# Swapping two of the seven products in a retention + PReLU kernel

## The chip, the cores and the metric

The kernel runs on one core of one Trainium2 chip. The metric is the device time of one execution in microseconds (us). Before the change the median of three runs is 198.67 us (197.17 to 201.42). The engines are named as the profile names them: PE multiplies matrices into PSUM banks, PEld loads its weights, DVE, ACT and POOL work element by element, SP starts most DMAs. Each engine takes its instructions in the order in which the program issues them.

## The reference

For each of 4 batches and 8 heads a retention state is carried through 768 steps; its output, as 3072 rows of 512 columns, goes through a two-layer network with a PReLU between:

```python
gamma = 1.0 - 2.0 ** (-5.0 - np.arange(H))
for t in range(S):                       # B, H, S, D = 4, 8, 768, 64
    state = gamma * state + outer(k[:, :, t], v[:, :, t])
    y[:, :, t] = scale * q[:, :, t] @ state
x = y.transpose(0, 2, 1, 3).reshape(B * S, H * D)
h = x @ w_in                             # 3072 x 512 @ 512 x 2048
g = np.maximum(h, 0) + alpha * np.minimum(h, 0)
out = g @ w_out                          # 3072 x 2048 @ 2048 x 512
```

## The kernel before, in words

The 3072 rows are cut into 6 blocks (0 to 5) of 512 rows, each of them four units of 128 rows. Retention makes xT of a block; the first layer multiplies it with w_in into `hps` banks, and ACT and DVE make the PReLU from these into `gt` (16 slices of 128 features by 512 rows, fp16). The second layer multiplies gt with w_out. Block 0 does that with plain products. Blocks 1 to 5 use `seven(n)`: gt and w_out are cut in two each way and a Strassen-like scheme (Winograd's) forms the four output quarters from seven half-size products. Each product is 16 matmuls of 128x256 (two row halves `t`, eight feature slices `f`).

The products need sums of quarters. Of w_out they are made once (`wsum[0]` to `wsum[3]`). Of gt they are made per block by `g_sums(n, part, which, engine)` (line 782): `which` 0 is `sm[0]`, 1 is `sm[1]`, which is `sm[0]` minus a quarter of gt, 2 is `third`, and 3 changes a quarter of gt in place. `part` is the half of the eight slices that is made, None both.

`seven(n)` (line 802) is a generator: each `yield` follows one matmul, and what stands between two products (a copy, an addition, a store) is issued when the generator is next resumed after the last matmul of a product. `kept(bank, tag)` (line 825) has ACT copy a whole PSUM bank to SBUF (line 827); `put` (line 833) has DVE add a bank to such a copy (line 839) and gives back a function that issues the store.

In the text, P1 to P7 are the products in the order of the kernel before:

- P1 into bank b, copied by `kept` as s1; P2 into bank a, added to s1 by `put`, first output quarter
- P3 adds `sm[1]` times `wsum[1]` to b, copied as u2
- P4 puts `sm[0]` times `wsum[0]` into bank c, which is the same bank as a
- P5 adds `third` times `wsum[2]` to b, copied as u3, second output quarter from c and u3
- P6 into bank d, third quarter; P7 adds to c, fourth quarter from c and u2

The four banks of the rotation are called k, k+1, k+2, k+3 after the counter `turns` (the next to be used; the first layer's `hps` have used them in turn). b is k, a and c are k+1, d is k+2. While `seven(n)` runs, the retention of the next block runs between its products, put there by hand with counts: `tick(gen, m)` issues the next m matmuls. In blocks 2 to 4 that is 34 matmuls, `masked` and sums on DVE for the first pair of units (`chain(pa)`, line 1348), 26 matmuls, the outputs of the first pair (`out_first`, line 1369, into banks k+2 and k+3; two small ACT copies called `seen`), the scores and states of the second pair and `out_second(pa)` (line 1381), in which two ACT copies `xT<-ya` and `xT<-yb` (line 608) empty these banks. After that come `chain(pb)` on DVE, 6 matmuls, casts and more ticks, and `out_first(pb)` (line 1403). Block 1 does the same with 64 matmuls ahead of its `out_first(pa)`. So in blocks 1 to 4 the 65th matmul of `seven`, with what is issued ahead of it, stands in the tick of 6 behind `out_second(pa)`. In block 5 nothing is left to interleave from the third product on.

Of the kernel before, what the change touches and what calls it, by code (L numbers as in the profile page):

```python
# [19 lines left out]
def kernel(  # L20
# [72 lines left out]
    def bank(i, name, dt=FP, n=512):  # L93
        return psp.tile([128, n], dt, tag=f"p{i % 4}", bufs=1, name=name)

    def ps(name, dt=FP, n=512, tag="pa"):
        if tag == "pb":
            turns[0] += 1
            return bank(turns[0] - 1, name, dt, n)
        return psp.tile([128, n], dt, tag=tag, bufs=4, name=name)  # L100
# [653 lines left out]
    gsum, wsum, third = {}, {}, []  # L754
# [27 lines left out]
    def g_sums(n, part, which, eng):  # L782
        if n not in gsum:
            gsum[n] = [
                sbp.tile([128, HF, 256], F16, tag=f"gs{i}", bufs=1, name=f"gs{n}{i}") for i in range(2)
            ]
        gt, sm = gts[n], gsum[n]
        lo, hi = (0, HF) if part is None else (4 * part, 4 * part + 4)
        f, f8 = slice(lo, hi), slice(HF + lo, HF + hi)
        t0, t1 = slice(0, 256), slice(256, 512)  # L790
        if which == 0:
            minus(eng, sm[0][:, f], gt[:, f, t1], gt[:, f8, t1], op=ADD)
        elif which == 1:
            minus(eng, sm[1][:, f], sm[0][:, f], gt[:, f, t0])
        elif which == 2:
            if not third:
                third.append(sbp.tile([128, HF, 256], F16, tag="ukq", bufs=2, name="third"))
            minus(eng, third[0][:, f], gt[:, f, t0], gt[:, f, t1])
        else:
            minus(eng, gt[:, f8, t0], gt[:, f8, t0], sm[1][:, f])  # L800

    def seven(n):
        gt, sm = gts[n], gsum[n]

        def product(bank, a, w, first=False):
            for t in range(2):
                for f in range(HF):
                    bk = bank[t] if isinstance(bank, list) else bank
                    nc.tensor.matmul(  # L809
                        out=bk[:, 256 * t : 256 * t + 256],  # L810
                        lhsT=a[:, f, 128 * t : 128 * t + 128],
                        rhs=w[:, f, :],
                        start=first and f == 0 and (t == 0 or bk is not bank),
                        stop=(f == HF - 1),
                        skip_group_check=True,
                    )
                    yield

        def A(i, j):
            return gt[:, HF * j : HF * j + HF, 256 * i : 256 * i + 256]  # L820

        def W(j, l):
            return w_out_all[:, HF * j : HF * j + HF, 256 * l : 256 * l + 256]

        def kept(bank, tag):
            t = sbp.tile([128, 512], FP, tag=tag, bufs=2, name="kept")
            nc.scalar.activation(out=t, in_=bank, func=COPY, bias=0.0, scale=1.0)  # L827
            return t

        end = n + 1 == NBLK  # L830


        def put(i, l, x, y, op=ADD, ts=(0, 1), store=None):
            os_sb = sbp.tile([128, d_model], FP, tag="os", bufs=5, name="os")
            parts = [slice(256 * t, 256 * t + 256) for t in ts]
            if not isinstance(x, list):
                parts, x = [slice(0, 512)], [x]
            for at in parts:
                nc.vector.tensor_tensor(  # L839
                    out=os_sb[:, at], in0=x[at.start // 256][:, at], in1=y[:, at], op=op  # L840
                )
            rows = slice(TB * n + 256 * i + 128 * ts[0], TB * n + 256 * i + 128 * ts[-1] + 128)
            return lambda: (store or (nc.scalar if end else nc.sync)).dma_start(
                out=out[rows, 256 * l : 256 * l + 256].rearrange("(t p) c -> p t c", p=128),
                in_=os_sb[:, 256 * ts[0] : 256 * ts[-1] + 256].rearrange(
                    "p (t c) -> p t c", c=256
                ),
            )

        k = turns[0]  # L850
        b, a = bank(k, "ops"), bank(k + 1, "ops")
        yield from product(b, A(0, 0), W(0, 0), True)
        s1 = kept(b, "um0")
        yield from product(a, A(0, 1), W(1, 0), True)
        store = put(0, 0, a, s1)
        yield from product(b, sm[1], wsum[1])
        u2 = kept(b, "um0")
        store()
        c = bank(k + 1, "ops")
        if end:  # L860
            c = [c, ps("ops")]
        yield from product(c, sm[0], wsum[0], True)
        yield from product(b, third[0], wsum[2])
        u3 = kept(b, "um1")
        store = put(1, 1, c, u3)
        d = bank(k + 2, "ops")
        turns[0] = k + 2
        yield from product(d, A(1, 1), wsum[3], True)
        store()
        store = put(1, 0, u3, d, SUB)  # L870
        if end:
            gen = product(c, A(0, 1), W(1, 1))
            for _ in range(HF):
                yield next(gen)
            store()
            put(0, 1, c, u2, ts=(0,), store=nc.sync)()
            yield from gen
            put(0, 1, c, u2, ts=(1,))()
        else:
            yield from product(c, A(0, 1), W(1, 1))  # L880
            store()
            late_stores.append(put(0, 1, c, u2))
# [391 lines left out]
    for n in range(1, NBLK):  # L1274
        more = n + 1 < NBLK
# [35 lines left out]
            pq = scores(us)  # L1311
            states(us)
        for p, w in (
            ((0, 1), (1, 0), (1, 1)) if n == 1 else ((None, 0), (None, 1)) if more else ((1, 0), (1, 1))
        ):
            g_sums(n, p, w, V)
        gen = seven(n)
        if not more:
            tick(gen, 4 * HF + 2)
# [127 lines left out]
```

## Time and profile before

| | |
|---|---|
| median of 3 runs | 198.67 us (197.17 to 201.42) |
| profiled execution | 198.98 us, span 197.0 us |
| busy: PE / PEld / DVE / ACT / POOL | 189.3 / 131.7 / 151.3 / 121.7 / 147.5 us |
| matmuls of `seven` (line 809) | 560, 273 ns each |
| granted clock of PE | 1.000 |

A row of the timeline reads: start in us from the span's start, duration in us, engine, line, operation, what it writes and reads, the shape, how many instructions are merged in the row, and in brackets the idle time of the engine before it and what ended that. Matmuls overlap, so the duration of one is longer than the step from one start to the next. The span leaves out 198.98 - 197.0 = 1.98 us that lie around the profiled instructions.

### The profile page before, as it was taken

The numbers are of one execution on the slowest core, as the hardware profiler recorded it, in microseconds if no ns is written. First come the engines' busy times: TensorE is split into PE (matmuls) and PEld (weight loads), VectorE is DVE, ScalarE is ACT, GpSimd is POOL, SyncE is SP. The second block draws the span as 40 slices with busy tenths as digits, with TensorE's granted clock in tenths as the row PEclk, the third lists the DMA queues.
The fourth block names the chain that finished last, engine by engine and source line by source line (L and its number), as shares of the span: only waits on it lengthen the run. The fifth ranks groups of instructions, "written<-read, shape, count | busy, mean of one in ns | idle before, by whom it ended". The sixth has DMA issues, their size and how long they took to land.

```text
span 197.0 us, 6461 instructions
## 1 busy us (share of the span) xinstructions
PE 189.3 (96%) x2668; PEld 131.7 (67%) x2668; DVE 151.3 (77%) x260; ACT 121.7 (62%) x272; POOL 147.5 (75%) x148
## 2 busy tenths in 40 slices
PE   7789899999999989999999999999999999999993
PEld 5657444557768878744688754788754888654882
DVE  2597889253999698588897879968879977799943
ACT  3368664349687863476458988749987433687120
POOL 3286788999996955999659999579999397589000
PEclk9999999999999999999999999999999999999999
DMA  6999999999999989899999999993890011200014
GB/s 168 310 336 350 404 396 296 332 358 179 210 230 148 214 257 272 196 215 299 196 231 228 226 185 265 237 221 93 113 263 2 3 57 63 100 3 0 2 57 160
DMA packets 92749, 38.78 MB, mean 197 GB/s; under 512 B 70176, under 2 KB 88624, under 8 KB 92720
## 3 DMA queue, kind: packets, MB, share of 16 engines
q1 hardware_dynamic: 91440, 37.36, 77.2%
q10 hardware_dynamic: 1280, 1.01, 1.5%
q8 instruction: 21, 0.34, 0.7%
q14 instruction: 8, 0.07, 0.1%
HBM read 27.35 MB, written 6.29 MB: 171 GB/s over the span
## 4 chain that ended last, share of the span: by engine, by line
PE 73%; SPq 10%; DMA 7%; POOL 6%; DVE 1%; issue 1%; POOLq 0%
PE ops L809 30%; PE hps L942 16%; PE hps L632 12%; PE hps L972 5%; SPq L340 4%; SPq L117 4%; DMA wi<-in_moe_w_in_dram 4%; PE ops L734 4%; POOL wsum L757 3%; DMA kqs<-in_q_dram 3%; PE ya L293 1%; PE yb L293 1%; POOL gs L757 1%; DVE gs L757 1%; POOL ukq L354 1%; PE sca L234 1%
## 5 line engine op out<-in xcount | busy, mean ns | idle before, releaser
L809 PEld LDWEIGHTS <-gt 128*128 128x128 f16 x320 | 30.6, 98 | 4.2
L942 PE MATMUL hps<-xT,win 128*128 128x512 f16 x144 | 33.0, 379 | 0.0
L929 DVE SCALAR_TENSOR_TENSOR gt<-hm,small,hps 128x512 f16<-128x512 f32 (+1 forms) x42 | 28.7, 706 | 5.1 <-ACT hm L925 3.8
L809 PE MATMUL ops<-wout,gt 128*128 128x256 f16 x240 | 28.4, 273 | 0.0
L925 ACT ACTIVATE hm<-hps 128x512 f32<-128x512 f32 x39 | 23.1, 593 | 6.1 <-PE hps L942 5.4
L632 PE MATMUL hps<-xT,win 128*128 128x512 f16 x112 | 24.7, 379 | 0.6 <-POOL win L1073 0.6
L137 POOL TENSOR_TENSOR kq<-kqs,tab 128x512 f16<-128x512 f32 x23 | 23.7, 1051 | 1.9 <-DMA kqs<-in_q_dram 1.9
L642 DVE SCALAR_TENSOR_TENSOR gt<-hm,small,hps 128x512 f16<-128x512 f32 x28 | 20.9, 748 | 3.8 <-ACT hm L641 0.9
L942 PEld LDWEIGHTS <-win 128*128 128x128 f16 x144 | 14.1, 98 | 14.5
L641 ACT ACTIVATE hm<-hps 128x512 f32<-128x512 f32 x28 | 16.7, 597 | 8.9 <-PE hps L632 8.6
L674 DVE SCALAR_TENSOR_TENSOR gt<-hm,small,hps 128x256 f16<-128x256 f32 x40 | 16.9, 476 | 5.0 <-ACT hm L669 5.0
L827 ACT ACTIVATE kept<-ops 128x512 f32<-128x512 f32 x15 | 9.0, 597 | 18.8 <-PE ops L809 18.7
L632 PEld LDWEIGHTS <-win 128*128 128x128 f16 x112 | 10.9, 98 | 13.6 <-POOL win L1073 1.1
L809 PE MATMUL ops<-wsum,gs 128*128 128x256 f16 x160 | 19.0, 273 | 0.7 <-DVE gs L757 0.7
L217 POOL TENSOR_TENSOR t<-ss,tab 128x256 f16<-128x256 f32 x13 | 8.7, 669 | 13.6 <-DVE ss L215 13.6
L757 POOL TENSOR_TENSOR gt<-gt,gs 128x1024 f16<-128x1024 f16 x8 | 17.0, 2126 | 2.2 <-DVE gs L757 2.2
L660 PE MATMUL hps<-xT,win 128*128 128x256 f16 x160 | 18.4, 273 | 0.0
L129 ACT ACTIVATE kq<-kqs,tab 128x64 f16<-128x64 f32 x72 | 18.0, 336 | 0.0
L660 PEld LDWEIGHTS <-win 128*128 128x128 f16 x160 | 15.4, 98 | 2.6 <-DVE xT L584 0.3
L809 PEld LDWEIGHTS <-gs 128*128 128x128 f16 x160 | 15.1, 98 | 3.0 <-DVE gs L757 1.0
L669 ACT ACTIVATE hm<-hps 128x512 f32<-128x512 f32 x20 | 11.8, 597 | 4.5 <-PE hps L660 4.4
L839 DVE TENSOR_TENSOR os<-ops,kept 128x512 f32<-128x512 f32 (+1 forms) x17 | 10.5, 624 | 5.0 <-ACT kept L827 3.7
(139 smaller groups left out, 391.5 us busy)
## 6 DMA issues: line engine op xcount, KB each, us to landing
out_dram<-os SPq DMA_DIRECT2D x20, 256.0 KB, 3.6
wi<-in_moe_w_in_dram SPq DMA_DIRECT2D x8, 512.0 KB, 8.6
wo<-in_moe_w_out_dram SPq DMA_DIRECT2D x8, 512.0 KB, 8.7
kqs<-in_k_dram SPq DMA_DIRECT2D x16, 256.0 KB, 4.4
kqs<-in_q_dram SPq DMA_DIRECT2D x16, 256.0 KB, 4.3
vs<-in_v_dram SPq DMA_DIRECT2D x16, 256.0 KB, 4.7
ku<-in_k_dram SPq DMA_DIRECT2D x4, 256.0 KB, 4.4
qu<-in_q_dram SPq DMA_DIRECT2D x4, 256.0 KB, 5.3
```

The lines of the kernel that those rows point to most:

```text
L129: eng.activation(out=kqs[u][:, a, h % 4, h // 4, :], in_=staged[u][nm][:, h, :], func=COPY, bias=0.0, scale=tab[:, H * a + h : H * a + h + 1],
L137: eng.tensor_tensor(out=kqs[u][:, a].rearrange("p i r d -> p r i d"), in0=staged[u][nm].rearrange("p (r i) d -> p r i d", i=4), in1=tab[:, ...
L632: nc.tensor.matmul(out=hps, lhsT=w_in_all[:, hp, 128 * ft : 128 * ft + 128], rhs=xT[n][:, :, hp, :], start=(hp == 0), stop=(hp == 3),)
L641: nc.scalar.activation(out=hm, in_=hps, func=RELU, bias=0.0, scale=-1.0)
L642: nc.vector.scalar_tensor_tensor(out=gt_at(n, ft, slice(0, TB)), in0=hm, scalar=oma_sb[:, ft : ft + 1], in1=hps, op0=MULT, op1=ADD,)
L660: nc.tensor.matmul(out=hps[:, 256 * (ft - f0) : 256 * (ft - f0) + 256], lhsT=w_in_all[:, hp, 128 * ft : 128 * ft + 128], rhs=xT[n][:, half ...
L674: nc.vector.scalar_tensor_tensor(out=gt_at(n, f, to), in0=hm[:, at], scalar=oma_sb[:, f : f + 1], in1=hps[:, at], op0=MULT, op1=ADD,)
L757: eng.tensor_tensor(out=out, in0=a, in1=b, op=op)
L809: nc.tensor.matmul(out=bk[:, 256 * t : 256 * t + 256], lhsT=a[:, f, 128 * t : 128 * t + 128], rhs=w[:, f, :], start=first and f == 0 and ( ...
L925: nc.scalar.activation(out=t, in_=src, func=RELU, bias=0.0, scale=-1.0)
L929: nc.vector.scalar_tensor_tensor(out=gt_at(n, f, cols), in0=hm, scalar=oma_sb[:, f : f + 1], in1=src, op0=MULT, op1=ADD,)
L942: nc.tensor.matmul(out=hps, lhsT=w_in_all[:, hp, 128 * ft : 128 * ft + 128], rhs=x[:, :, hp, :], start=(hp == 0), stop=(hp == 3),)
```

## The change

The third and fourth of the seven products change places: the product with `sm[0]` comes third, the one with `sm[1]` fourth. The second product goes into bank k+2 in place of k+1, so that c, still in k+1, no longer shares its bank with a. The store of the first quarter is issued after the new third product, the copy u2 after the new fourth, which is now directly ahead of the product with `third` that adds to the same bank. In block 1 the half sums of gt on DVE are issued in the order (1, 0), (0, 1), (1, 1), as (part, which), where they were (0, 1), (1, 0), (1, 1).

```diff
         k = turns[0]
-        b, a = bank(k, "ops"), bank(k + 1, "ops")
+        b, a = bank(k, "ops"), bank(k + 2, "ops")
         yield from product(b, A(0, 0), W(0, 0), True)
         s1 = kept(b, "um0")
         yield from product(a, A(0, 1), W(1, 0), True)
         store = put(0, 0, a, s1)
-        yield from product(b, sm[1], wsum[1])
-        u2 = kept(b, "um0")
-        store()
         c = bank(k + 1, "ops")
         if end:
             c = [c, ps("ops")]
         yield from product(c, sm[0], wsum[0], True)
+        store()
+        yield from product(b, sm[1], wsum[1])
+        u2 = kept(b, "um0")
         yield from product(b, third[0], wsum[2])
         u3 = kept(b, "um1")
...
         for p, w in (
-            ((0, 1), (1, 0), (1, 1)) if n == 1 else ((None, 0), (None, 1)) if more else ((1, 0), (1, 1))
+            ((1, 0), (0, 1), (1, 1)) if n == 1 else ((None, 0), (None, 1)) if more else ((1, 0), (1, 1))
         ):
             g_sums(n, p, w, V)
```

## The prediction

> **What bounds the kernel now.** I read the page first: busy times, then the chain that ended last.
>
> ```profile
> PE 189.3 (96%) x2668; PEld 131.7 (67%) x2668; DVE 151.3 (77%) x260; ACT 121.7 (62%) x272; POOL 147.5 (75%) x148
> PE 73%; SPq 10%; DMA 7%; POOL 6%; DVE 1%; issue 1%; POOLq 0%
> ```
>
> PE is busy nearly all the time and is 73% of the chain. Busy matmuls can hide pauses, so I read next what PE waited for, and then the chain in order of time, first and last pieces from the first `seven` on.
>
> ```profile
> PE ops L809 <- DVE gs L757: 0.7, 1, 0.7
> ...
> 70.84 3.23 PE ops L809 x28
> ...
> 181.69 12.26 PE ops L809 x112
> 193.98 0.42 DVE os L839
> ```
>
> Line 809 waits once, for a sum of gt, and the chain starts anew at that wait's end (70.84). From there to 193.98, where DVE adds the last quarter, all of the chain's pieces are PE's. No other engine ends a wait of PE there. Two rules follow: time that PE loses between 70.84 and 193.98 is added to the end, unless something later on PE waits less for it; and time is won only at the one wait.
>
> **What the swap puts on PE.** Before, P4 (into c) lies between P3 and P5, which both add to bank b. ACT's copy u2 of b runs under P4. After, P5 stands directly behind the product whose sum u2 copies, and adds to the same bank, so PE has to wait for the copy. In blocks 1 to 4 there is more: u2 is issued when the generator is resumed for the 65th matmul, which is behind `out_second(pa)`, so on ACT's queue it stands behind the two xT copies. Block 2, PE and then ACT, in the timeline:
>
> ```profile
> 99.78 3.22 PE L809 MATMUL ops<-wsum,gs 128*128 128x256 f16 x28
> 104.11 0.61 PE L809 MATMUL ops<-wsum,gs 128*128 128x256 f16 x4
> 104.56 2.00 PE L809 MATMUL ops<-wsum,third 128*128 128x256 f16 x16
> ```
>
> ```profile
> 101.73 0.60 ACT L827 ACTIVATE kept<-ops 128x512 f32<-128x512 f32 x1 [0.99 <-PE ops L809]
> 104.32 0.60 ACT L608 ACTIVATE xT<-ya 128x512 f16<-128x512 f32 x1 [0.54 <-PE yb L293]
> 104.81 0.59 ACT L608 ACTIVATE xT<-yb 128x512 f16<-128x512 f32 x1
> 105.29 1.15 ACT L150 ACTIVATE vx<-vs 128x512 f16<-128x512 f32 x2
> ```
>
> The 28 are P3 and 12 of P4 (a step of (3.22 - 0.27)/27 = 0.109 us, one product 1.75), the retention of the next block stands from 103.0 to 104.11, the last 4 of P4 follow, and P5 starts at 104.56 without a pause. u2, at 101.73 before, takes the place on ACT that the vx casts have now: 105.29, 0.60 long, done at 105.89. Its own product is done before 105, so ACT's queue decides. The hand-over to PE I take from block 1's wait below (sum done 70.78, matmul at 70.84): 0.06. P5 starts at 105.95 in place of 104.56: **+1.39**.
>
> Blocks 3 and 4, each with ACT's xT copy and P5:
>
> ```profile
> 133.57 0.59 ACT L608 ACTIVATE xT<-yb 128x512 f16<-128x512 f32 x1
> 134.04 1.15 ACT L150 ACTIVATE vx<-vs 128x512 f16<-128x512 f32 x2
> 133.30 1.91 PE L809 MATMUL ops<-wsum,third 128*128 128x256 f16 x16
> ...
> 162.23 0.59 ACT L608 ACTIVATE xT<-yb 128x512 f16<-128x512 f32 x1
> 162.02 1.91 PE L809 MATMUL ops<-wsum,third 128*128 128x256 f16 x16
> ```
>
> Block 3: u2 from 134.04 to 134.64, P5 at 134.70 in place of 133.30, **+1.40**. Block 4: nothing follows the copy at once; the next place is 0.48 after its start, as in block 2 (105.29 - 104.81), 162.71; P5 at 162.71 + 0.60 + 0.06 = 163.37 in place of 162.02, **+1.35**.
>
> Block 5 has no retention between, so u2 waits only for its product:
>
> ```profile
> 185.04 3.66 PE L809 MATMUL ops<-wsum,gs 128*128 128x256 f16 x32
> 188.54 1.91 PE L809 MATMUL ops<-wsum,third 128*128 128x256 f16 x16
> 190.28 1.91 PE L809 MATMUL ops<-wsum,gt 128*128 128x256 f16 x16
> ...
> 187.05 0.60 ACT L827 ACTIVATE kept<-ops 128x512 f32<-128x512 f32 x1 [2.96 <-PE ops L809]
> 190.48 0.60 ACT L827 ACTIVATE kept<-ops 128x512 f32<-128x512 f32 x1 [2.84 <-PE ops L809]
> ```
>
> P3's successor starts at 185.04 + 16 x 0.109 = 186.79, its copy at 187.05, 0.26 later; P5's successor at 190.28, its copy at 190.48, 0.20 later. The pause is 0.23 + 0.60 + 0.06 = **+0.89**.
>
> **Block 1, where something is won and lost.** POOL, DVE and PE around the wait, then PE and DVE in `out_first(pa)`, then ACT and P5:
>
> ```profile
> 66.61 2.12 POOL L757 TENSOR_TENSOR gs<-gt 128x1024 f16<-128x1024 f16 x1
> 68.77 0.69 DVE L757 TENSOR_TENSOR gs<-gs,gt 128x1024 f16<-128x1024 f16 x1 [1.69 <-POOL gs L757]
> 69.38 0.68 DVE L757 TENSOR_TENSOR gs<-gt 128x1024 f16<-128x1024 f16 x1
> 70.09 0.69 DVE L757 TENSOR_TENSOR gs<-gs,gt 128x1024 f16<-128x1024 f16 x1
> 69.56 0.60 PE L809 MATMUL ops<-wsum,gs 128*128 128x256 f16 x4
> 70.84 3.23 PE L809 MATMUL ops<-wsum,gs 128*128 128x256 f16 x28 [0.68 <-DVE gs L757]
> ...
> 74.10 0.41 DVE L203 TENSOR_TENSOR t<-t,sta 128x256 f16<-128x256 f16 x1
> 74.34 0.20 PE L293 MATMUL ya<-kt,t 64*64 64x64 f16 x2
> 74.56 0.22 PE L293 MATMUL yb<-kt,t 64*64 64x64 f16 x2
> ...
> 75.50 0.60 ACT L608 ACTIVATE xT<-ya 128x512 f16<-128x512 f32 x1 [0.41 <-PE yb L293]
> 75.99 0.59 ACT L608 ACTIVATE xT<-yb 128x512 f16<-128x512 f32 x1
> 75.68 0.72 PE L809 MATMUL ops<-wsum,third 128*128 128x256 f16 x5
> ```
>
> DVE idles 1.69 until POOL's half of sm[0] (68.73), then makes three half sums in a row; PE gets four matmuls in and stops, its fifth starting 70.84 - (69.56 + 4 x 0.109) = 0.84 late. The new order puts the half that needs nothing of POOL into the idle time, so sm[1] is whole one sum earlier (70.09 - 69.38 = 0.71); and the product with sm[0] comes first, for which both halves are there by 68.73. PE's wait goes whole: -0.84. What is late next is DVE's chain: PE stops at 74.34 for a state sum that ends at 74.51 and goes on at 74.56, and the sums ahead of it on DVE come only 0.71 earlier. So of the 0.84, **-0.71** reaches `out_second(pa)`. Then the new wait: the xT copies move to 74.79 and 75.28, u2 to 75.76, done at 76.36, P5 at 76.42 in place of 75.68: block 1 nets **+0.74**.
>
> **Costs that I put at nothing.** P2's new bank k+2 held the last `hps` but one. P2 reads the gt slices that are made from all the `hps`, so it waits for these already; the same covers c in k+1. Bank k+2 is then wanted by `out_first(pa)`, after `put` has read it:
>
> ```profile
> 100.41 0.68 DVE L839 TENSOR_TENSOR os<-ops,kept 128x512 f32<-128x512 f32 x1
> ```
>
> Done at 101.09, while PE reaches `out_first` at 103.0: 1.9 of cover. If it went, PE would wait there by the difference. The store stays at the same matmul count, on the same queue (SP; ACT in block 5, where its quarter has long been added). In blocks 2 to 5 the earlier need of sm[0] wins nothing, as PE waits for no sum there. Moving u2 delays behind it on ACT the casts vx (in blocks 2 and 3) and u3; u3 waits for P5 anyway, and the casts feed the block after.
>
> **Sum.** 0.74 + 1.39 + 1.40 + 1.35 + 0.89 = +5.77. On the profiled execution 198.98 + 5.77 = 204.75; that execution is 0.31 above the median, so 204.44, which I give as **204.5 us**. Lower bound of the unknown: u2 waits only for its product everywhere (0.89 five times) and the whole 0.84 is won, +3.61, so 202.3. Upper bound: the two xT copies and u2 each take a full 0.60 in blocks 1 to 4 with no overlap (104.32 + 1.80 + 0.06 = 106.18, 0.23 more in each of four), and block 1 wins nothing (0.71 more): +7.40, so 206.1.
>
> **Rivals.**
>
> *Absorbed downstream (about 199).* The pause moves PE only. If `out_first(pb)` waits for DVE and POOL anyway, blocks 1 to 4 pay nothing.
>
> ```profile
> 105.88 0.62 POOL L217 TENSOR_TENSOR t<-ss,tab 128x256 f16<-128x256 f32 x1
> 106.53 0.42 DVE L203 TENSOR_TENSOR t<-t,sta 128x256 f16<-128x256 f16 x1 [0.18 <-POOL t L217]
> 108.45 0.22 PE L293 MATMUL za<-kt,t 64*64 64x64 f16 x2
> ```
>
> It decides if the last operand comes after PE does. Block 2's last are done at 106.95, and PE arrives at 108.45, 1.50 later: the slack lies the wrong way. Full absorption would give -0.71 + 0.89 = +0.18, 198.67 + 0.18 = 198.9. This is the case that ends on the other side: not slower. 0.06.
>
> *Only the product's own copy (about 202.3).* If ACT gets to u2 as soon as the product is done, each pause is 0.89, the lower bound above. Against it stand the xT copies at 104.32 and 104.81, ahead of u2 in program order. 0.08.
>
> *The pauses cost the clock (about 213).* PE now pauses in every `seven`. The nearest row is the stretch behind block 1's pause of 0.84, which ends at 70.84:
>
> ```profile
> 71.00:76.00 5.00, 4.97 (x159) 4.24 (x158) 4.50 (x9) 1.90 (x7) 3.58 (x3) 1.00 1.19 290
> ```
>
> Its last three columns are the granted clock, DMA's share and GB/s: the clock stays at 1.00. If the product behind each of five pauses ran at half rate, each would cost 1.75 more: 204.5 + 8.7 = 213.2. [...] 0.03.
>
> *Forecast, within 202.3 to 206.1:* 0.83.
>
> **Range and chances.** The three runs of before spread from 1.5 below to 2.75 above their median, so I widen the bounds a little, to **202.0 to 206.8**. The measurement can tell about 2% from no change, 3.97 us, so the line is at 202.6. The forecast case lies below it in about 0.05 of its 0.83, the case at 202.3 for half of its 0.08, and the absorbed case wholly, of which 0.02 may come out faster by the scatter of the runs: slower 0.78 + 0.04 + 0.03 = 0.85, same 0.13, faster 0.02.
>
> **What would show it.** In the profile after, the waits should have a new group: PE line 809 waiting for ACT kept, line 827, 5 times, some 6.4 us in total (1.45 in block 1, where the -0.71 comes off elsewhere), the longest near 1.4. On ACT, u2 directly behind `xT<-yb` in blocks 1 to 4. The wait for DVE gs gone from PE. `out_first(pb)` without a wait. PE's granted clock 1.00. The prediction is wrong if P5 starts without waiting, if u2 stands ahead of the xT copies, or if PE's waits further on shrink by what the pauses add.

## The result and the profile after

The changed kernel takes 204.86 us (median of 6 executions, 204.04 to 224.41) against 199.06 (6 executions, 197.17 to 202.36). A second set, of 7 and 11 executions, gives 205.15 against 199.13. By the medians it is slower by 5.8 and 6.0 us. The ratios, 1.0329 (95% interval 1.0251 to 1.0407) and 1.0285 (1.0235 to 1.0335), leave out the slow executions of both kernels, so they are not the quotients of these medians.

The execution that was profiled with the result, the one of 224.41, ran at a granted clock of 0.85 from some 6 us on, far ahead of the change, and of 0.95 from some 196 us on (columns of the stretch: PE, PEld, DVE, ACT, POOL busy, granted clock, DMA share, GB/s):

```profile
20.00:40.00 20.00, 20.00 (x89) 9.29 (x88) 13.60 (x21) 10.74 (x19) 17.65 (x26) 0.85 1.04 361
```

The readings below are therefore from another execution of the same kernel, 205.35 us, span 203.4, clock 1.000. First its chain by engine (a q marks an engine's sequencer; issue is time for which the profile shows no wait), then two groups of what PE waited for (us in all, times, longest):

```profile
PE 70%; DVE 8%; SPq 6%; DMA 5%; ACT 3%; POOL 3%; issue 3%; ACTq 0%; POOLq 0%
```

```profile
PE ops L809 <- ACT kept L827: 5.4, 5, 1.2
...
PE yb L293 <- DVE t L203: 0.7, 1, 0.7
```

ACT, which was no link of the chain, now is 3% of it. The five waits for the copy are there, one in each block, and the wait for a sum of gt is gone; a wait of 0.7 for a state sum (`t`) has grown in its place. A wait counts from the modelled end of the last matmul, some 0.17 us behind the next matmul's place (a duration of 0.27 less a step of 0.11). So the delays below, taken from start to start, are longer than 5.4 in all.

Block 2 in the timeline, PE and then ACT:

```profile
101.27 3.22 PE L809 MATMUL ops<-wsum,gs 128*128 128x256 f16 x28
...
105.60 0.61 PE L809 MATMUL ops<-wsum,gs 128*128 128x256 f16 x4
107.44 1.91 PE L809 MATMUL ops<-wsum,third 128*128 128x256 f16 x16 [1.22 <-ACT kept L827]
```

```profile
105.81 0.60 ACT L608 ACTIVATE xT<-ya 128x512 f16<-128x512 f32 x1 [0.54 <-PE yb L293]
106.31 0.59 ACT L608 ACTIVATE xT<-yb 128x512 f16<-128x512 f32 x1
106.78 0.60 ACT L827 ACTIVATE kept<-ops 128x512 f32<-128x512 f32 x1
107.26 1.16 ACT L150 ACTIVATE vx<-vs 128x512 f16<-128x512 f32 x2
```

u2 stands directly behind the two xT copies, ends at 107.38, and the product with `third` starts 0.06 later. Block 5 has the product's own copy alone:

```profile
190.58 3.66 PE L809 MATMUL ops<-wsum,gs 128*128 128x256 f16 x32
...
194.33 0.60 ACT L827 ACTIVATE kept<-ops 128x512 f32<-128x512 f32 x1 [4.70 <-PE ops L809]
```

For every run I took two measures that do not depend on what happens ahead of block 1. For blocks 2 to 5 it is the time from the first matmul of the third product to the first of the product with `third` (2: 107.44 - 101.27 = 6.17). For block 1 it is the time from the end of POOL's half of sm[0] to the first matmul with `third`, since block 1 hangs on that half:

| from start to start, us | block 1 | 2 | 3 | 4 | 5 |
|---|---|---|---|---|---|
| before | 6.95 | 4.78 | 4.82 | 4.83 | 3.50 |
| after | 8.08 | 6.17 | 6.22 | 6.18 | 4.40 |
| difference | +1.13 | +1.39 | +1.40 | +1.35 | +0.90 |
| predicted | +0.74 | +1.39 | +1.40 | +1.35 | +0.89 |

### The profile page after: what moved, and what is told of

It reads as the page before. It is cut to its first block, busy times and chain, and to the rows that moved or that the text cites. A ratio compares the mean times of both kernels' runs of the same rounds, so it can differ in the third digit from the quotient of the medians.

```text
span 222.5 us, 6461 instructions
## 1 busy us (share of the span) xinstructions
PE 210.0 (94%) x2668; PEld 138.6 (62%) x2668; DVE 151.4 (68%) x260; ACT 121.7 (55%) x272; POOL 147.3 (66%) x148
## 4 chain that ended last, share of the span: by engine, by line
PE 87%; SPq 4%; DMA 3%; ACT 3%; issue 1%; POOL 0%; DVE 0%; ACTq 0%
PE ops L809 31%; PE hps L942 16%; PE hps L632 13%; PE hps L660 9%; PE ops L734 6%; PE hps L972 5%; SPq L340 4%; DMA wi<-in_moe_w_in_dram 3%; PE ops L696 2%; ACT xT L608 1%; ACT kept L827 1%; PE ya L293 1%; PE yb L293 1%; PE sca L234 1%; PE sta L188 1%
## 5 line engine op out<-in xcount | busy, mean ns | idle before, releaser
L942 PE MATMUL hps<-xT,win 128*128 128x512 f16 x144 | 37.2, 414 | 0.0
L809 PEld LDWEIGHTS <-gt 128*128 128x128 f16 x320 | 32.3, 103 | 6.2
L929 DVE SCALAR_TENSOR_TENSOR gt<-hm,small,hps 128x512 f16<-128x512 f32 (+1 forms) x42 | 29.2, 708 | 9.8 <-ACT hm L925 9.0
L809 PE MATMUL ops<-wout,gt 128*128 128x256 f16 x240 | 31.5, 291 | 0.0
L925 ACT ACTIVATE hm<-hps 128x512 f32<-128x512 f32 x39 | 23.2, 596 | 10.7 <-PE hps L942 10.7
L632 PE MATMUL hps<-xT,win 128*128 128x512 f16 x112 | 28.4, 422 | 0.0
L942 PEld LDWEIGHTS <-win 128*128 128x128 f16 x144 | 15.0, 104 | 17.1
L641 ACT ACTIVATE hm<-hps 128x512 f32<-128x512 f32 x28 | 16.7, 597 | 13.0 <-PE hps L632 13.0
L632 PEld LDWEIGHTS <-win 128*128 128x128 f16 x112 | 11.9, 107 | 15.7
L660 PE MATMUL hps<-xT,win 128*128 128x256 f16 x160 | 21.2, 294 | 0.1
L809 PE MATMUL ops<-wsum,gs 128*128 128x256 f16 x160 | 21.0, 291 | 0.0
L660 PEld LDWEIGHTS <-win 128*128 128x128 f16 x160 | 16.1, 104 | 4.7 <-ACT win L1087 0.5
L809 PEld LDWEIGHTS <-gs 128*128 128x128 f16 x160 | 16.3, 103 | 3.0
L809 PE MATMUL ops<-wsum,third 128*128 128x256 f16 x80 | 10.5, 289 | 5.6 <-ACT kept L827 5.6
```

The costliest lines, as they stand in the source:

```text
L632: nc.tensor.matmul(out=hps, lhsT=w_in_all[:, hp, 128 * ft : 128 * ft + 128], rhs=xT[n][:, :, hp, :], start=(hp == 0), stop=(hp == 3),)
L641: nc.scalar.activation(out=hm, in_=hps, func=RELU, bias=0.0, scale=-1.0)
L660: nc.tensor.matmul(out=hps[:, 256 * (ft - f0) : 256 * (ft - f0) + 256], lhsT=w_in_all[:, hp, 128 * ft : 128 * ft + 128], rhs=xT[n][:, half ...
L809: nc.tensor.matmul(out=bk[:, 256 * t : 256 * t + 256], lhsT=a[:, f, 128 * t : 128 * t + 128], rhs=w[:, f, :], start=first and f == 0 and ( ...
L925: nc.scalar.activation(out=t, in_=src, func=RELU, bias=0.0, scale=-1.0)
L929: nc.vector.scalar_tensor_tensor(out=gt_at(n, f, cols), in0=hm, scalar=oma_sb[:, f : f + 1], in1=src, op0=MULT, op1=ADD,)
```

## The experiments

"The stretch" is the time from block 1's first product to the start of DVE's last addition; it is 127.92 before.

**The changed kernel again.**

> The changed kernel once more, for a profile at granted clock 1.00. My theory: PE waits five times for ACT's copy u2 at the start of the product with third, 1.45, 1.39, 1.40, 1.35 and 0.89 us, 6.5 in all; the stretch from the first product of block 1 to DVE's last addition, 127.9 us before (66.06 to 193.98), becomes 133.7. If the pauses cost the clock, it shows below 1.00 behind a pause and the stretch is longer than 134.5; if they are absorbed, the stretch stays near 128.

Measured: five pauses as in the table; the clock 1.000; the stretch 200.42 - 66.00 = 134.42, 0.7 over the 133.7. From the first product with `third` to the end of the stretch it is 123.23 in place of 118.30, +4.93 where the pauses of blocks 2 to 5 make 5.04: all but 0.11 of them reaches the end. The surplus lies in block 1:

```profile
66.97 2.14 POOL L757 TENSOR_TENSOR gs<-gt 128x1024 f16<-128x1024 f16 x1
67.09 2.56 DVE L757 TENSOR_TENSOR gs<-gt 128x1024 f16<-128x1024 f16 x1
69.57 1.28 DVE L757 TENSOR_TENSOR gs<-gs,gt 128x1024 f16<-128x1024 f16 x2
74.63 0.22 PE L293 MATMUL yb<-kt,t 64*64 64x64 f16 x2 [0.66 <-DVE t L203]
77.19 1.91 PE L809 MATMUL ops<-wsum,third 128*128 128x256 f16 x16 [1.05 <-ACT kept L827]
```

These are rows of POOL, DVE and PE. The half sum that was moved beside POOL's took 2.56 us where it takes 0.68 alone. It ends 0.54 behind POOL's (69.65, 69.11). So sm[1] is whole 1.74 behind POOL's end, not 2.05 as before: 0.31 won, not the 0.71 that I had put down. PE runs ahead to `out_first(pa)` and waits 0.66 there for DVE's chain. The other part of the surplus is that POOL itself came later in this execution, 0.97 behind block 1's first product and not 0.55.

**The copy ahead of the xT copies.** If the pauses of blocks 1 to 4 come from u2's place on ACT, issuing it earlier and giving PE the retention to do meanwhile must remove them.

```diff
-        def product(bank, a, w, first=False):
+        def product(bank, a, w, first=False, done=None):
...
+                    if done and t == 1 and f == HF - 1:
+                        done()
                     yield
...
-        yield from product(b, sm[1], wsum[1])
-        u2 = kept(b, "um0")
+        u2 = []
+        yield from product(b, sm[1], wsum[1], done=lambda: u2.append(kept(b, "um0")))
+        u2 = u2[0]
...
-                tick(gen, 26)
+                tick(gen, 30)
...
-            tick(gen, 6)
+            tick(gen, 2 if n > 1 else 6)
```

> The changed kernel, with u2 issued together with the last matmul of its product, and in blocks 2 to 4 the whole product issued ahead of out_first (30 in place of 26 matmuls, then 2 in place of 6): ACT now meets u2 ahead of the two xT copies, and PE has the retention of the next block (1.1 us in block 2) to do while ACT copies. My theory: the pauses of blocks 1 to 4 go, block 5's 0.9 stays, block 1's gain of 0.7 stays: the stretch from block 1's first product to the last addition 127.9 - 0.7 + 0.9 = 128.1 us, the time about 199. Rival (the swap or the bank costs by itself, whatever ACT does): the time stays at 204 to 205.

Measured: 201.11 us, ratio to before 1.0103 (1.0056 to 1.0150); the stretch 195.57 - 67.31 = 128.26. ACT and PE in block 2, and the one wait that is left:

```profile
103.72 0.60 ACT L829 ACTIVATE kept<-ops 128x512 f32<-128x512 f32 x1 [2.74 <-PE ops L809]
...
105.00 0.60 ACT L608 ACTIVATE xT<-ya 128x512 f16<-128x512 f32 x1 [0.54 <-PE yb L293]
```

```profile
104.80 1.92 PE L809 MATMUL ops<-wsum,third 128*128 128x256 f16 x16
```

```profile
PE ops L809 <- ACT kept L829: 0.7, 1, 0.7
```

Blocks 2 to 4 take 4.77, 4.81 and 4.82, as before the change, block 5 still 4.40. Block 1 has no pause either: 75.91 - 67.31 = 8.60 from its first product to the one with `third`, against 9.62 before the change, where PE waited for a sum. The order of products and the banks are those of the changed kernel, so neither costs anything by itself in these blocks. The stretch is near the 128.1 that I expected; the time is some 2 us over it. In the profiled execution (200.51 us) that surplus is not behind block 1's first product; where it comes from in the others, with code ahead of block 1 that is the same, stays open.

**Also block 5 in the old order.**

```diff
+        if end:
+            yield from product(b, sm[1], wsum[1], done=lambda: u2.append(kept(b, "um0")))
         yield from product(c, sm[0], wsum[0], True)
         store()
-        yield from product(b, sm[1], wsum[1], done=lambda: u2.append(kept(b, "um0")))
+        if not end:
+            yield from product(b, sm[1], wsum[1], done=lambda: u2.append(kept(b, "um0")))
```

> As copy_early, and in block 5 the product with sm[1] is third again and the one with sm[0] fourth. My theory: no wait for ACT's copy is left, the stretch is 127.9 - 0.7 = 127.2 us and the time 198.0 to 198.5, 0.9 below copy_early. Rival (block 5's pause is hidden by DVE and the stores at the end): the same as copy_early.

Measured: 199.06, ratio 0.9999 (0.9955 to 1.0042), the stretch 194.02 - 66.30 = 127.72. Block 5 is back at 3.49, blocks 2 to 4 at 4.77, 4.82, 4.81, and PE waits for no copy. So the pauses are the whole loss of these blocks. The gain of 0.7 that I expected is not left at the end: block 1 took 8.60 from its first product to the one with `third`, 1.02 less than before, but from there to the last addition it is 194.02 - 74.90 = 119.12, 0.82 more than before. POOL began 0.70 ahead of block 1's first product here, so the 8.60 is no mark of the new order; the kernel before shows it too in an execution with POOL as early (its second profile, below).

**One copy more, one copy less ahead of the product.** The suspected cost doubled:

```diff
+        kept(b, "um1")
         u2 = kept(b, "um0")
```

> The changed kernel with one more copy of the same bank on ACT directly ahead of u2, in every block: the suspected cost is made longer by one copy, about 0.5 us (0.60, overlapped by 0.1 with the next). My theory: each of five pauses grows by 0.5, the time by 2.5 us, to 207.3; PE's waits for ACT's copy are some 9 us. Rival (the pause is not ACT's copy, or it is absorbed further on): less than 1 us.

Measured: 209.43, ratio 1.0530 (1.0474 to 1.0587). From start to start the blocks take 8.57, 6.66, 6.72, 6.66 and 4.83: 0.49, 0.49, 0.50, 0.48 and 0.43 more than after, 2.4 in all, as expected. ACT in block 2, in the timeline, and the group of PE's waits:

```profile
109.49 1.09 ACT L827 ACTIVATE kept<-ops 128x512 f32<-128x512 f32 x2
```

```profile
PE ops L809 <- ACT kept L827: 8.2, 5, 1.9
```

The time rose by more than that, about 4.5 us over the changed kernel. In the profiled execution the rest is PE's clock, which I come back to at the end.

The other way, with one xT copy taken off ACT:

```diff
         if z is None:
+            if X == 1:
+                nc.vector.tensor_copy(out=to, in_=src)
+                return
             nc.scalar.activation(out=to, in_=src, func=COPY, bias=0.0, scale=1.0)
```

> The changed kernel, with the second of the two xT copies of out_second(pa) done by DVE in place of ACT in blocks 1 to 4: u2 has one copy less ahead of it on ACT. My theory: in blocks 2 to 4 u2 starts when its product is done, and the pause falls from 1.4 to 0.9 us; in block 1 it falls by 0.5: the time falls by 2.0 us to about 202.8, if DVE's chain for the second pair, which comes 0.7 later, stays inside its slack of 1.5 us. Rival (ACT's queue plays no part, the pause is the product's own copy and the hand-overs): no change, 204.9.

Measured: 203.15, ratio 1.0220 (1.0150 to 1.0289). The blocks take 7.59, 5.65, 5.73, 5.73 and 4.40: 0.49, 0.52, 0.49 and 0.45 less than after, and nothing less in block 5, which has no xT copy. Block 2 in the timeline, ACT and then PE:

```profile
104.98 0.59 ACT L830 ACTIVATE kept<-ops 128x512 f32<-128x512 f32 x1
```

```profile
105.63 1.91 PE L812 MATMUL ops<-wsum,third 128*128 128x256 f16 x16 [0.71 <-ACT kept L830]
```

Each copy on ACT ahead of the product is worth one step of ACT, 0.43 to 0.52 us here, in both directions. The rival without ACT's queue falls.

**The order of the half sums alone, and the swap without it.** The changed kernel with block 1's sums in the old order:

```diff
-            ((1, 0), (0, 1), (1, 1)) if n == 1 else ((None, 0), (None, 1)) if more else ((1, 0), (1, 1))
+            ((0, 1), (1, 0), (1, 1)) if n == 1 else ((None, 0), (None, 1)) if more else ((1, 0), (1, 1))
```

> The changed kernel with block 1's half sums in the old order. My theory: the wait for a sum still shrinks, as the product with sm[0] needs only the first two of the three half sums, but DVE's chain behind them comes no earlier, so the 0.7 is not won: the stretch from block 1's first product to the last addition is 0.7 us longer than that of the changed kernel, 134.4. Rival (the whole gain comes from the product's new place): the same as the changed kernel, 133.7.

Measured: 204.96 us (one execution). From POOL's end to the product with `third` block 1 takes 8.39, against 8.08 after and 6.95 before: the new order of sums is worth 0.31, not 0.7, and the swap alone costs 1.44 in block 1, where I had 1.45. The stretch, 200.04 - 66.03 = 134.01, is shorter than that of the changed kernel all the same, because POOL's sum came 0.20 behind the first product here and 0.97 there. It is no fit measure for block 1.

The kernel before with only the new order of sums:

```diff
-            ((0, 1), (1, 0), (1, 1)) if n == 1 else ((None, 0), (None, 1)) if more else ((1, 0), (1, 1))
+            ((1, 0), (0, 1), (1, 1)) if n == 1 else ((None, 0), (None, 1)) if more else ((1, 0), (1, 1))
```

> The kernel before with nothing changed but block 1's order of half sums on DVE. My theory: sm[1] is whole 0.7 us earlier, PE waits for it at most 0.15, DVE's chain comes 0.7 earlier: the stretch 127.2 us, the time 198.3. Rival (the sum beside POOL runs as slowly as it is moved forward, or another wait takes its place): the stretch stays 127.9.

Measured: 199.45 against 199.13, ratio 1.0019 (0.9983 to 1.0055), the stretch 127.96. Block 1 takes 6.64 from POOL's end, 0.31 less than before; again the sum beside POOL is stretched (timeline, POOL and DVE):

```profile
66.32 2.13 POOL L757 TENSOR_TENSOR gs<-gt 128x1024 f16<-128x1024 f16 x1
```

```profile
66.84 2.16 DVE L757 TENSOR_TENSOR gs<-gt 128x1024 f16<-128x1024 f16 x1
```

It ends at 69.00, 0.55 behind POOL's 68.45. In seven profiled executions with this order (without that of 224.41) the sum started 0.12 to 1.70 us behind POOL's and took 2.56 to 0.97 us, but always ended 0.54 or 0.55 behind it, as if it did its work after POOL's. My expectation of 0.7 fell, and the rival's "as slowly as it is moved forward" nearly holds. Of the 0.31 nothing is left at the end either: from the product with `third` to the last addition it is 193.75 - 75.09 = 118.66, 0.36 more than before.

**The sum taken off POOL.** If that is the cause, DVE is better off making all four halves itself. The kernel before, with

```diff
-    g_sums(1, 0, 0, G)
...
-            ((0, 1), (1, 0), (1, 1)) if n == 1 else ((None, 0), (None, 1)) if more else ((1, 0), (1, 1))
+            ((0, 0), (1, 0), (0, 1), (1, 1)) if n == 1 else ((None, 0), (None, 1)) if more else ((1, 0), (1, 1))
```

> The kernel before, with block 1's first half of sm[0] made by DVE in place of POOL: the four half sums in the order (0,0), (1,0), (0,1), (1,1) on DVE. Theory (a DVE sum stands still while POOL makes one): with no sum of POOL beside them the four take 0.6 to 0.7 us each from 67.1, the last ends near 69.8 in place of 70.8, PE waits for none, and from block 1's first product to its product with third it is 8.7 us in place of 9.6; time 0.9 us (0.5%) below that of the kernel before. Rival (the sum was slow by itself, or another wait takes the place): (1,0) takes over 1.5 us again, or the stretch stays above 9.3.

Block 1 in the timeline, DVE and then PE:

```profile
66.24 1.28 DVE L757 TENSOR_TENSOR gs<-gt 128x1024 f16<-128x1024 f16 x2
67.45 1.28 DVE L757 TENSOR_TENSOR gs<-gs,gt 128x1024 f16<-128x1024 f16 x2
```

```profile
68.81 3.66 PE L809 MATMUL ops<-wsum,gs 128*128 128x256 f16 x32
73.92 1.92 PE L809 MATMUL ops<-wsum,third 128*128 128x256 f16 x16
```

Four sums in 2.49 us, the third product without a pause, 73.92 - 65.31 = 8.61 from block 1's first product to the one with `third` in place of 9.62, and the stretch 192.16 - 65.31 = 126.85, 1.07 less than before. That is as expected. The time is 198.84 against 198.98, ratio 0.9982 (0.9940 to 1.0024): a gain of 0.5% lies inside that interval, and so does none. It is the shortest stretch of all, but no version here is shown to beat the kernel before.

**The bank alone.**

```diff
-        b, a = bank(k, "ops"), bank(k + 1, "ops")
+        b, a = bank(k, "ops"), bank(k + 2, "ops")
```

> The kernel before with nothing changed but the second product's bank, k+2 in place of k+1. My theory: nothing moves, PE waits as before, the stretch from block 1's first product to the last addition is 127.9 us. Rival (the bank is held by something): a new wait of PE at the second product or at out_first(pa).

PE's wait for sums in block 1, and POOL's half sum in the timeline:

```profile
PE ops L809 <- DVE gs L757: 1.6, 2, 0.9
```

```profile
68.18 2.12 POOL L757 TENSOR_TENSOR gs<-gt 128x1024 f16<-128x1024 f16 x1
```

Measured: 200.97 us (one execution). There is no wait at the second product or at `out_first`. The stretch is 196.02 - 66.49 = 129.53 and not 127.9: POOL came 1.69 behind the first product here, and PE waited 1.6 for the sums. From POOL's end block 1 takes 6.94, as before (6.95). The bank does nothing; the expectation of the stretch missed, as it took POOL's arrival for fixed.

**The kernel before again.**

> The kernel before, unchanged, for a second profile of it: how much does block 1 differ between executions of the same program? In the profile at hand POOL starts its half of sm[0] 0.55 us after block 1's first product. If POOL's start there depends on the loads ahead of it, it lies elsewhere, and from the end of POOL's sum to the product with third it is still 6.95 us; from that product to the last addition 118.3 us, up to 0.5 more with pauses of issue.

Measured: 203.91 us, a long one: block 1's first product starts at 70.85 and not at 66.06, so PE lost its time ahead of `seven`. A transfer held it up there, and behind that wait the granted clock was 0.50 for some 3.4 us (one of PE's waits, and a stretch):

```profile
PE sca L483 <- DMA ukT<-ukq: 1.8, 1, 1.8
```

```profile
58.00:59.00 1.00, 1.00 (x3) 0.30 (x2) 1.00 (x3) 1.00 (x6) 1.00 (x1) 0.50 1.07 242
```

From block 1's third product to the one with `third` PE does not wait at all (timeline):

```profile
74.35 3.66 PE L809 MATMUL ops<-wsum,gs 128*128 128x256 f16 x32
79.45 1.92 PE L809 MATMUL ops<-wsum,third 128*128 128x256 f16 x16
```

79.45 - 70.85 = 8.60 from the first product, the time without a pause. From POOL's end it is 7.13 and not 6.95, since here PE's own work ends last. From there to the last addition it is 198.94 - 79.45 = 119.49, over the 118.8 that I allowed: PE waited 0.7 for an addition in block 2. So the wait whose removal I counted as block 1's gain is not in every execution of the kernel before. It was missing here, where POOL began 0.65 ahead of block 1's first product.

**More executions of the changed kernel, for the clock.**

> The changed kernel, unchanged, in more executions, for the granted clock: with the second copy PE's granted clock fell to 0.50 for some 6 us behind block 1's pause of 1.87 us, and all of its executions show a mean of 0.984 to 0.992. Theory (the changed kernel's pauses, up to 1.4 us, are too short for that): its executions show 0.998 to 1.000 about as often as those of the kernel before, and the ratio is 1.029 again, 5.8 us. Rival (its pauses too set the clock off at times): means near 0.99 in more than a third of its executions, and these 1.7 us or more longer than the rest.

Measured: the ratio 1.0285 given above. Two of seven executions show a mean clock of 0.992 (207.69 and 208.74 us), the other five 1.000 (204.33 to 205.50). With the earlier ones, and without that of 224.41, it is two of 13. Of 64 executions of the kernel before beside these runs four show 0.991, and so do, at 0.990 or 0.991, three of the twelve of the kernel with the sum taken off POOL, which has none of the new pauses. The rival's "more than a third" isn't reached, but "about as often" isn't shown either: these are too few to tell. What happens in such an execution stands at the end.

## Why the prediction was right, point by point

- **PE from 70.84 on sets the end, and what PE loses there is added.** Right. +4.93 from block 1's product with `third` to the last addition against pauses of 5.04; the absorbed case, at 198.9, falls with it. The waits in the profile, 5.4 us, make some 6.2 with 0.17 added to each of the five, against some 6.4 put down.
- **P5 has to wait for u2, and u2 stands behind the xT copies.** Right in place and in size: 1.39, 1.40, 1.35, 0.89 predicted; 1.39, 1.40, 1.35, 0.90 measured. A copy more or less on ACT moves each pause by 0.43 to 0.52, and with u2 ahead of the xT copies they are gone. The case with the product's own copy alone (202.3) falls for blocks 2 to 4, and is what block 5 shows.
- **Block 1 wins 0.84 at the sum, of which 0.71 is left.** The mis-sized term. I put down "The new order puts the half that needs nothing of POOL into the idle time, so sm[1] is whole one sum earlier". PE's wait for the sum did go, and PE did stop at the state sum next, as put down; but the half sum did not run in the idle time. By its times it stood still until POOL's was done (2.56 us in place of 0.68, ending 0.54 behind it), so that sm[0] was whole at 69.65 and not by POOL's end. Sums and states came 0.31 earlier, so that block 1 nets 1.44 - 0.31 = +1.13 from POOL's end, not +0.74. Why the sum was held up isn't shown. I had the evidence in the profile before and passed over it: a DVE sum beside a POOL sum is in it twice (last section). With 0.55 behind POOL's end for the first sum and two more steps of 0.6, sm[1] would have come out at 1.75 behind POOL's end; 1.74 was measured.
- **The costs put at nothing.** Right: no wait for bank k+2 or k+1 shows, with the change or with the bank alone, and none that the stores or the casts would cause.
- **The sum.** 5.77 predicted, 1.13 + 1.39 + 1.40 + 1.35 + 0.90 = 6.17 by the traces, 5.8 and 6.0 by the medians. The intervals of the two ratios, 5.0 to 8.1 us and 4.7 to 6.7 us, hold both sums, so the times can't tell them apart. That the first median difference meets 5.77 so closely, with a term of it mis-sized by 0.39, is luck. What block 1 loses also differs between executions, since its wait for a sum depends on when POOL comes: in the eleven profiled executions in which POOL makes the half (without that of 224.41), it began between 0.77 ahead of block 1's first product and 1.69 behind it.
- **The clock.** Given 0.03 as a case for the time; the median shows none of it. Half rate behind each of the five pauses was my assumption, and no run shows it: with the second copy the clock was at 0.50 behind block 1's pause alone, where the product took 3.37 us in place of 1.74, and at 1.00 from 83 us on. A stretch at half clock behind block 1's pause is also in one profile of the changed kernel (below), which I had not allowed for beside the forecast.

## What to carry to other kernels

When two products that add to the same PSUM bank are made neighbours, the copy between them moves onto PE's path with all that its engine has queued ahead of it (0.90 us here for the copy alone, 1.39 with two xT copies ahead of it): find its new place in that queue, not only its duration. A gap in DVE's timeline is not always free time: a sum moved into the time in which POOL makes another sum gained 0.31 us of 0.71 here. And where the time ahead of a stretch scatters by more than the effect, measure the effect between two events inside the stretch.

## What the runs showed of the hardware

**DVE's half sum of gt, started beside POOL's in block 1, ended 0.54 or 0.55 us behind it.** That was so in seven executions, with starts from 0.12 to 1.70 us behind POOL's; with no POOL sum beside them such sums step every 0.6 (69.38 - 68.77 = 0.61 before). The profile before has it with other sums, in block 1:

```profile
73.01 0.61 POOL L217 TENSOR_TENSOR t<-ss,tab 128x256 f16<-128x256 f32 x1
73.28 0.89 DVE L757 TENSOR_TENSOR third<-gt 128x1024 f16<-128x1024 f16 x1
74.88 0.68 DVE L757 TENSOR_TENSOR third<-gt 128x1024 f16<-128x1024 f16 x1
75.04 0.99 POOL L217 TENSOR_TENSOR t<-ss,tab 128x256 f16<-128x256 f32 x1 [1.42 <-DVE ss L215]
```

The first `third` sum starts beside POOL's `t`, takes 0.89 in place of 0.68, and ends at 74.17, again 0.55 behind POOL's end (73.62). At 74.88 DVE starts first, and it is POOL's sum that grows, to 0.99 from 0.61. A DVE sum with an operand in PSUM was not held up in the same profile: `m` from the bank `sca` took 0.68 and ended at 72.77, ahead of the end of the POOL sum beside it (73.06); all sixteen sums of `m` took 0.68:

```profile
70.93 2.13 POOL L757 TENSOR_TENSOR gt<-gt,gs 128x1024 f16<-128x1024 f16 x1 [2.20 <-DVE gs L757]
72.09 0.68 DVE L248 TENSOR_TENSOR m<-sca,mi 128x512 f16<-128x512 f32 x1
```

**With a pause of 1.87 us in block 1 the granted clock fell to 0.50.** With the second copy, granted clock and matmuls in and behind block 1's pause, which lasts from 75.19 to 77.06:

```profile
75.00:77.00 2.00, 0.19 (x18) 0.17 (x8) 1.39 (x5) 2.00 (x4) 0.94 (x2) 0.77 1.16 265
77.00:80.00 3.00, 2.94 (x14) 2.01 (x14) 0.99 (x3) 0.01 (x1) 3.00 (x3) 0.50 1.04 233
80.00:83.00 3.00, 3.00 (x16) 2.06 (x14) 0.69 (x1) 0.60 (x1) 3.00 (x5) 0.52 0.91 207
83.00:90.00 7.00, 7.00 (x104) 4.38 (x103) 4.12 (x7) 3.58 (x8) 6.50 (x8) 1.00 1.07 292
```

```profile
77.06 3.57 PE L809 MATMUL ops<-wsum,third 128*128 128x256 f16 x16 [1.87 <-ACT kept L827]
80.43 2.79 PE L809 MATMUL ops<-wsum,gt 128*128 128x256 f16 x13
```

If the clock went from 1.00 to 0.50 in one step, the mean of 0.77 puts the fall some 0.9 us into the pause, and the 0.52 of 80 to 83 its end at some 82.9. P5 takes 3.37 to the next product's start and not 1.74, and P6 3.76 where the changed kernel has 2.54: 2.85 us, beside the 2.4 of the longer pauses. All four executions of that kernel show means of 0.984 to 0.992. In the changed kernel the same was caught once in a profile, behind a pause of 1.38 in block 1:

```profile
78.00:80.00 2.00, 2.00 (x11) 1.45 (x10) 1.11 (x3) 0.00 (x0) 2.00 (x2) 0.50 1.01 225
```

It was at 0.50 from 77.8 to 81.2 there. The second profile of the kernel before has such a stretch too, 56.1 to 59.5, behind the wait of 1.8 for a transfer; so it doesn't take the change. The pauses of 1.2 to 1.7 in blocks 2 to 4 did not set it off in these profiles: the 16 matmuls of P5 took 1.91 us behind each of them, and 3.57 and 3.50 behind those of 1.87 and 1.38 in block 1. Behind a pause of 1.38 in block 1 with the sums in the old order they took 1.91. In block 1 a wait for DVE and then 64x64 matmuls alone stand ahead of the pause, in blocks 2 to 4 four matmuls of a product come between; whether that decides isn't shown.
